# Attention and ELU layers in one kernel: one block transpose for two heads, chunk outputs and small elementwise steps moved to ScalarE

## The chip, the cores and the metric

The kernel runs on one core of a Trainium2 chip. The metric is the device time of one execution in microseconds; the median of three runs is what is compared. The engines are named as in the profile: PE is TensorE, PEld its weight loads, DVE is VectorE, ACT is ScalarE, POOL is GpSimd, SP is SyncE (it only issues DMAs here).

## What is computed

Four batches of eight heads, 768 positions, 64 values a head: attention over a window of 16 positions to either side, joined with 24 block summaries (the maximum of each 32 keys, the mean of each 32 values), then a two-layer network with ELU over all 3072 rows.

```python
k_sum = k.reshape(B, H, nb, 32, D).max(axis=3)
v_sum = v.reshape(B, H, nb, 32, D).mean(axis=3)
scores_l = np.where(abs(i - j) < 16, scale * q @ k.T, -1e9)
scores_s = scale * q @ k_sum.T + log(32)
s = concatenate([scores_l, scores_s], -1)
a = exp(s - s.max(-1)); a = a / (a.sum(-1) + 1e-9)
x = (a @ concatenate([v, v_sum])).reshape(3072, 512)
h = x @ w_in                                   # 512 -> 2048
g = where(h > 0, h, exp(minimum(h, 0)) - 1)
out = g @ w_out                                # 2048 -> 512
```

## The kernel before

The network's matmuls run in a format that keeps fewer bits of a float32, so each operand is split into a high part and the rest, and each product is made of three (high by high, high by rest, rest by high). Rows are worked in six chunks of 512 (`CH`). For each chunk there are sixteen steps `f`, one for each 128 of the 2048 hidden values; step number `n` is `16 * c + f`. A step has these parts:

- `layer1` (L613): 12 matmuls of 512 columns into `h`, from `xh` and `xl`.
- the ELU: `exp_of` (L635) on ScalarE makes `e`; `below` (L640) on VectorE takes min(e, 1) - 1; `above` (L643) on VectorE adds max(h, 0).
- `split_high` (L647) copies `e` to `gh` on ScalarE, `split_rest` (L652) makes `gl` on GpSimd.
- `layer2` (L667): 12 matmuls into the four output banks `o0` to `o3`, from `gh` and `gl`. On TensorE it is issued one step late: the first layer of step n stands ahead of the second layer of step n - 1. At a chunk's last step each bank is finished by itself, copied out and stored (L698 to L700): outputs 0 and 2 by ScalarE, 1 and 3 by VectorE, into borrowed buffers (`cv` twice, `sm`, and the queries' `qbd`).

Attention is worked in groups `g`, twenty of them after those of the start: four steps for a group, which covers two pairs of heads and a third of a batch's rows. At step 2 of four, TensorE makes the values of group g (`group_values`, L570, out of the transposed weights `pt`) and the scores of group g + 1 (`group_scores`, L515). Then the softmax of g + 1 follows for each of its two heads h: `lowest` (L163) on VectorE adds the mask and finds the extreme, `exps` (L173) is four ScalarE passes that also give the sums `z`, `reciprocals` (L181) adds 1e-9 and inverts on VectorE, and `scale_rows` (L185) multiplies on GpSimd. In steps 3, 0 and 1 `group_blocks` (L555) transposes the weights `sm` to `pt` on VectorE, 32 x 32 blocks, 32 instructions a group (11, 11 and 10), issued after the step's `above`. Groups of the first chunk use TensorE for this instead.

Ahead of later batches the block summaries are reduced on VectorE (`summary`, L493) from key and value rows that SyncE loads into two `cv` buffers (`load_summary`, L476); queries and key and value windows of the coming group are loaded by the same queue (`load_group`, L441).

In the first chunk the weights arrive as 64-bit floats and are converted (`Conversion`, L127): a GpSimd pass (`X`), a ScalarE pass (`M`), two VectorE passes (`S`), a ScalarE copy for the high part (`H`, L154) and a GpSimd pass for the rest (`L`, L157). The order of all engines in that chunk is written out by hand in the table `FIRST`, a word for each operation: `E.6` is the exponential of step 6, `ts.6` its `below`, `stt.6` its `above`, `G.6` and `gl.6` its splits, `gz.1.0` the reciprocals of group 1, head 0. After the table, TensorE and SyncE keep the order of the code, and the order on VectorE, ScalarE and GpSimd is made by a scheduler, with `issue_after` as a bound.

Of the kernel before, what the change touches and what calls it, by code (L numbers as in the profile page):

```python
# [26 lines left out]
P = 128  # L27
# [43 lines left out]
    gz.4.0 gz.4.1 gn.4.0 gn.4.1 gb.4.0.8  # L71
# [4 lines left out]
def attn_elu_ffn(ctx: ExitStack, tc: tile.TileContext, qT, kT, vT, v, w_in, w_out, out):  # L76
# [29 lines left out]
    mask = const.tile([P, 3, KC], F32, name="mask")  # L106

# [92 lines left out]
    def new_x(c):  # L200
        xs[c] = (att.tile([P, NP, CH], F32R, tag="xh", name="xh"), att.tile([P, NP, CH], F32R, tag="xl", name="xl"))
# [16 lines left out]
    def first_units():  # L218
# [3 lines left out]
        new_x(0)  # L222
# [18 lines left out]
        v_t = [att.tile([P, UW, row], F32, tag=t, name=f"v{t}") for t in ("xh", "xl")]  # L241
# [295 lines left out]
    def group_low(g, h):  # L537
        th = units[2 * g][0] % NTH
        wide = att.tile([P, UW, P], F32, tag="sm", name="sm")
        sm_of[g, h] = wide[:, :, 0:KC]  # L540
        if g >= NP:
            wide_of[g, h] = wide
            nc.gpsimd.memset(wide[:, :, KC:P], 0.0)
# [8 lines left out]
    def group_transposes(g, h):  # L552
        t_of[g, h] = transposes(sm_of.pop((g, h)), f"a{h}")

    def group_blocks(g, first, end):  # L555

        for i in range(first, end):
            h, (k, q) = i // 16, (x * BLK for x in divmod(i % 16, 4))
            if i % 16 == 0:
                del sm_of[g, h]  # L560
                pt_of[g, h] = att.tile([P, UW, P], F32, tag="pt", name="pt")
            nc.vector.transpose(out=pt_of[g, h][k:k + BLK, :, q:q + BLK], in_=wide_of[g, h][q:q + BLK, :, k:k + BLK])  # L562
            if i % 16 == 15:
                del wide_of[g, h]

    def group_copy(g, h, copy=nc.scalar.copy):
        pt_of[g, h] = att.tile([P, UW, P], F32, tag="pt", name="pt")
        copy(out=pt_of[g, h][0:KC], in_=t_of.pop((g, h))[0:KC])

    def group_values(g):  # L570
# [71 lines left out]

    def above(e, h_ps):  # L643
# [23 lines left out]
    def layer2(c, f):  # L667
# [188 lines left out]
```

## Time and profile before

| | us |
|---|---|
| median of three runs | 620.43 |
| lowest, highest | 617.85, 623.69 |
| the profiled execution | 618.44 |
| its span | 616.7 |
| PE busy | 603.7 |
| DVE busy | 422.4 |
| ACT busy | 256.1 |
| POOL busy | 253.1 |

The profile is of one execution. The span runs from its first to its last instruction; the difference to the execution's own time lies around it. A busy time is the union of an engine's instructions. A timeline row has the start, the length, the engine, the line and the operation, with x and a count where several are joined, and in brackets the idle time before it and what ended that.

### The profile page before, as it was taken

To read this page: it belongs to the slowest core of one execution; us is meant where nothing else is said; L and a number is where in the kernel's file an instruction comes from. 1 tells how busy PE (TensorE), PEld (TensorE's weight loads), DVE (VectorE), ACT (ScalarE), POOL (GpSimd) and SP (SyncE) were. 2 spreads that over 40 slices of the span, in tenths; PEclk is the share of its full clock that TensorE was granted. 3 is DMA by queue.
4 is the path that set the end of the run, shared out by engine and by line. 5 is a ranking of instruction groups with operands and counts; after the bars stand their busy time and mean duration, and the time that the engine had idled before them with its cause. 6 is when DMAs were issued, how large, how long until landed. Compare 5 with 4: busy or idle time off the path is not lost.

```text
span 616.7 us, 11558 instructions
## 1 busy us (share of the span) xinstructions
PE 603.7 (98%) x4123; PEld 490.4 (80%) x4123; DVE 422.4 (68%) x1365; ACT 256.1 (42%) x713; POOL 253.1 (41%) x298
## 2 busy tenths in 40 slices
PE   8999999998999999999999999999999999999997
PEld 6778778886888877888887888888788888888885
DVE  7789987777868878668688697686786774321122
ACT  5858776752332432433424424324243242322222
POOL 4999899842332323323323323233234232122221
PEclk9999999999999999999999999999999999999999
DMA  8998962213105145311053231501311000100001
GB/s 318 332 384 266 306 238 56 59 58 96 48 1 142 53 119 151 97 33 32 2 157 101 74 107 40 143 7 40 111 52 40 2 2 0 69 0 2 1 0 68
DMA packets 63553, 58.65 MB, mean 95 GB/s; under 512 B 22648, under 2 KB 54904, under 8 KB 63496
## 3 DMA queue, kind: packets, MB, share of 16 engines
q1 hardware_dynamic: 60184, 52.02, 27.9%
q10 hardware_dynamic: 3312, 5.90, 2.6%
q8 instruction: 32, 0.52, 0.3%
q14 instruction: 25, 0.20, 0.1%
HBM read 50.82 MB, written 6.29 MB: 93 GB/s over the span
## 4 chain that ended last, share of the span: by engine, by line
PE 67%; DVE 14%; ACT 3%; DMA 2%; issue 2%; SPq 1%; DVEq 0%; ACTq 0%
PE o L674 28%; PE h L621 27%; DVE pt L562 7%; PE h L632 3%; PE o L664 3%; PE o_ps L585 3%; ACT sm L177 2%; PE s L534 2%; DVE e L644 2%; DVE e L641 2%; DMA n<-in_kT_dram 1%; DVE ks L498 1%; DMA vw<-in_v_dram 1%; DVE sh L145 1%; DVE vst L498 1%
## 5 line engine op out<-in xcount | busy, mean ns | idle before, releaser
L654 POOL TENSOR_TENSOR gl<-e,gh 128x512 fp32r<-128x512 f32 x96 | 123.5, 1287 | 239.1 <-issue 133.9
L621 PE MATMUL h<-xh,w 128*128 128x512 f32 x640 | 212.3, 393 | 0.0
L674 PE MATMUL o<-w,gh 128*128 128x512 f32 x648 | 164.5, 390 | 4.0 <-DVE ot L699 2.1
L562 DVE STREAM_TRANSPOSE pt<-sm 32x128 f32<-32x128 f32 x512 | 154.9, 302 | 7.9
L674 PEld LDWEIGHTS o<-w,gh 128*128 128x128 f32 x648 | 121.2, 188 | 31.1 <-DVE ot L699 3.4
L621 PEld LDWEIGHTS h<-xh,w 128*128 128x128 f32 x640 | 120.1, 188 | 27.3 <-issue 2.4
L621 PE MATMUL h<-xl,w 128*128 128x512 f32 x320 | 124.6, 389 | 0.0
L637 ACT ACTIVATE e<-h 128x512 f32<-128x512 f32 x96 | 57.0, 594 | 162.0 <-PE h L621 151.9
L649 ACT CAST gh<-e 128x512 fp32r<-128x512 f32 x96 | 59.6, 621 | 123.4 <-DVE e L644 123.4
L641 DVE TENSOR_SCALAR e<-e 128x512 f32<-128x512 f32 x96 | 46.2, 481 | 92.2 <-ACT e L637 90.5
L674 PE MATMUL o<-w,gl 128*128 128x512 f32 x324 | 89.7, 390 | 0.0
L674 PEld LDWEIGHTS o<-w,gl 128*128 128x128 f32 x324 | 60.8, 188 | 13.0 <-POOL gl L654 0.3
L621 PEld LDWEIGHTS h<-xl,w 128*128 128x128 f32 x320 | 60.1, 188 | 12.0
L177 ACT ACTIVATE sm<-sm,mx 128x120 f32<-128x120 f32 x160 | 61.0, 383 | 19.0 <-DVE mx L169 19.0
L644 DVE SCALAR_TENSOR_TENSOR e<-h,e 128x512 f32<-128x512 f32 x96 | 66.4, 691 | 3.2
L186 POOL TENSOR_TENSOR sm<-sm,z 128x480 f32<-128x480 f32 x40 | 43.2, 1082 | 61.7 <-DVE z L183 53.3
L157 POOL TENSOR_TENSOR w<-cv,w 128x512 fp32r<-128x512 f32 x32 | 41.8, 1320 | 5.3 <-ACT w L154 4.5
L632 PE MATMUL h<-xh,w 128*128 128x512 f32 x120 | 40.5, 399 | 0.0
L599 DVE TENSOR_TENSOR xl<-o_ps,xh 128x256 fp32r<-128x256 f32 x40 | 15.1, 419 | 33.1 <-ACT xh L592 33.1
L169 DVE CUSTOM_DVE_ANT_0 sm<-s,mask 128x120 f32<-128x120 f32 x160 | 34.0, 278 | 1.9 <-PE s L534 1.8
L664 PE MATMUL o<-w,gh 128*128 128x512 f32 x120 | 32.1, 394 | 0.9 <-ACT gh L649 0.9
L177 ACT ACTIVATION_READ_ACCUMULATOR sm<-sm,mx 128x1 f32 x160 | 29.9, 187 | 0.0
(111 smaller groups left out, 529.1 us busy)
## 6 DMA issues: line engine op xcount, KB each, us to landing
raw_w<-in_w_in_dram SPq DMA_DIRECT2D x16, 512.0 KB, 8.1
raw_w<-in_w_out_dram SPq DMA_DIRECT2D x16, 512.0 KB, 9.1
qbd<-in_qT_dram SPq DMA_DIRECT2D x20, 256.0 KB, 2.8
out_dram<-ot ACTq DMA_DIRECT2D x15, 256.0 KB, 2.1
kw<-in_kT_dram SPq DMA_DIRECT2D x24, 144.0 KB, 3.5
vw<-in_v_dram SPq DMA_DIRECT2D x24, 144.0 KB, 3.3
n<-in_kT_dram SPq DMA_DIRECT2D x16, 192.0 KB, 2.4
n<-in_vT_dram SPq DMA_DIRECT2D x16, 192.0 KB, 2.3
```

The costliest lines, as they stand in the source:

```text
L177: nc.scalar.activation(out=sm[:, t, :], in_=sm[:, t, :], func=AF.Exp, bias=mx[:, t, :], scale=-1.0, accum_out=z[:, t, :])
L186: nc.gpsimd.tensor_tensor(out=sm, in0=sm, in1=z.broadcast_to([P, UW, KC]), op=ALU.mult)
L562: nc.vector.transpose(out=pt_of[g, h][k:k + BLK, :, q:q + BLK], in_=wide_of[g, h][q:q + BLK, :, k:k + BLK])
L621: nc.tensor.matmul(h_ps, w[:, a, cols], bb[:, cc, :], start=(k == 0), stop=(k == 3 * NCC - 1))
L632: nc.tensor.matmul(h_ps, w[:, lo, cc * P:(cc + 1) * P], bb[:, cc, :], start=(lo, cc, i) == (0, 0, 0), stop=(lo, cc) == (1, NCC - 1))
L637: nc.scalar.activation(out=e, in_=h_ps, func=AF.Exp)
L641: nc.vector.tensor_scalar(out=e, in0=e, scalar1=1.0, scalar2=-1.0, op0=ALU.min, op1=ALU.add)
L644: top = nc.vector.scalar_tensor_tensor(out=e, in0=h_ps, scalar=0.0, in1=e, op0=ALU.max, op1=ALU.add)
L649: nc.scalar.copy(out=gh, in_=e)
L654: nc.gpsimd.tensor_tensor(out=gl, in0=e, in1=gs[(c, f)][0].bitcast(F32), op=ALU.subtract)
L664: nc.tensor.matmul(o_acc[0][s], gs[(0, f)][a][:, s * P:(s + 1) * P], w[:, bb, :], start=(f, part) == (0, 0), stop=False)
L674: nc.tensor.matmul(o_acc[c][s], a[:, s * P:(s + 1) * P], w[:, bb, :], start=first and f == 0, stop=last and f == NF - 1)
```

## The change

It has five parts. One block transpose covers both heads: `sm` and `pt` become single tiles that hold both heads of a group, a transposition has 256 elements for each partition and there are 16 a group (6, 5 and 5; in a chunk's first step they are issued after the copy of output 1). At chunk ends ScalarE copies outputs 0, 2 and 3, VectorE output 1, all into the `xh` buffer of the finished chunk, and the `x` buffers get a tag for even and for odd chunks. The 1e-9 is added by a ScalarE pass with a bias tile `tiny`. The ELU of steps 6 and 7 is made of a ScalarE pass `gap`, relu(1 - e), and one VectorE pass `larger`, max(-gap, h). `tiny` is first the tile of the activation that warms ScalarE up.

```diff
-    M.15 ge.1.0 S.14 w.21 L2a.5 L2b.5 S.15 E.6 w.22 H.14 L2c.5 X.17 ts.6 H.15 L.14 L1h.7 w.23 M.16 gz.1.0 stt.6
+    M.15 ge.1.0 S.14 w.21 L2a.5 L2b.5 S.15 E.6 gap.6 w.22 H.14 L2c.5 X.17 H.15 L.14 L1h.7 w.23 M.16 gz.1.0 larger.6
...
     def normalize(sm, z):
-        reciprocals(z)
+        nc.vector.reciprocal(out=z, in_=z)
         scale_rows(sm, z)
...
-        xs[c] = (att.tile([P, NP, CH], F32R, tag="xh", name="xh"), att.tile([P, NP, CH], F32R, tag="xl", name="xl"))
+        xs[c] = [att.tile([P, NP, CH], F32R, tag=f"{t}{c % 2}", name=t, bufs=1) for t in ("xh", "xl")]
...
-        warm = const.tile([P, 1], F32, name="warm")
-        nc.vector.memset(warm, 0.0)
-        nc.scalar.activation(out=warm, in_=warm, func=AF.Exp)
+        nc.vector.memset(tiny, 0.0)
+        nc.scalar.activation(out=tiny, in_=tiny, func=AF.Exp)
+        nc.vector.memset(tiny, 1e-9)
...
     def group_exps(g, h):
-        z_of[g, h] = exps(sm_of[g, h], mx_of.pop((g, h)))
+        z_of[g, h] = z = exps(sm_of[g, h], mx_of.pop((g, h)))
+        nc.scalar.activation(out=z, in_=z, func=AF.Identity, bias=tiny)
...
     def group_blocks(g, first, end):
+        if first == 0:
+            for h in range(2):
+                del sm_of[g, h]
+            pt_of[g] = att.tile([P, 2, UW, P], F32, tag="pt", name="pt", bufs=1)
+        src, dst = (a.rearrange("p h t k -> p (h t) k") for a in (wide_of[g], pt_of[g]))
         for i in range(first, end):
-            h, (k, q) = i // 16, (x * BLK for x in divmod(i % 16, 4))
...
-            nc.vector.transpose(out=pt_of[g, h][k:k + BLK, :, q:q + BLK], in_=wide_of[g, h][q:q + BLK, :, k:k + BLK])
+            k, q = (slice(x * BLK, (x + 1) * BLK) for x in divmod(i, P // BLK))
+            nc.vector.transpose(out=dst[k, :, q], in_=src[q, :, k])
...
+    def gap(e):
+        nc.scalar.activation(out=e, in_=e, func=AF.Relu, bias=1.0, scale=-1.0)
+    def larger(e, h_ps):
+        nc.vector.scalar_tensor_tensor(out=e, in0=e, scalar=-1.0, in1=h_ps, op0=ALU.mult, op1=ALU.max)
...
             if not last_chunk:
-                if t < 2:
-                    ot = ffn.tile([P, DO], F32, tag="cv", name="ot", bufs=2)
...
-                (nc.vector.tensor_copy if t % 2 else nc.scalar.copy)(out=ot, in_=o_acc[c][t])
-                nc.scalar.dma_start(out=out[r:r + P, :], in_=ot)
+                if t == 1:
+                    copied = nc.vector.tensor_copy(out=ots[:, t, :], in_=o_acc[c][t]).ins
+                else:
+                    nc.scalar.copy(out=ots[:, t, :], in_=o_acc[c][t])
+                nc.scalar.dma_start(out=out[r:r + P, :], in_=ots[:, t, :])
...
-            if step != 2 and n < 4 * NG - 1:
+            if n % NF and step != 2 and n < 4 * NG - 1:
                 with tc.issue_after(turn):
                     if step == 3:
-                        group_blocks(g + 1, 0, 11)
-                    elif step == 0:
-                        group_blocks(g, 8 if g == NP else 11, 22)
+                        group_blocks(g + 1, 0, 6)
                     else:
-                        group_blocks(g, 22, 32)
+                        group_blocks(g, *(6, 11) if step == 0 else (8 if g == NP else 11, 16))
...
-                layer2(*divmod(n - 1, NF))
+                copied = layer2(*divmod(n - 1, NF))
+            if n % NF == 0 and g < NG:
+                with tc.issue_after(copied):
+                    group_blocks(g, *(0, 8) if g == NP else (6, 11))
```

VectorE at the end of the second chunk, before (L641 and L644 are the ELU's passes, `ot` and `qbd_70` the borrowed output buffers):

```order
L562 STREAM_TRANSPOSE pt<-sm 32x4x32 x11
L641 TENSOR_SCALAR e<-e 128x512
L644 SCALAR_TENSOR_TENSOR e<-h,e 128x512
L562 STREAM_TRANSPOSE pt<-sm 32x4x32 x11
L699 COPY ot<-o_2009 128x512
L699 COPY qbd_70<-o_2011 128x512
L641 TENSOR_SCALAR e<-e 128x512
```

The same place after (L652 and L663 are the ELU's passes, `ots` is the output tile in the `xh` buffer):

```order
L577 STREAM_TRANSPOSE pt<-sm 32x8x32 x6
L652 TENSOR_SCALAR e<-e 128x512
L663 SCALAR_TENSOR_TENSOR e<-h,e 128x512
L712 COPY ots<-o_1980 128x512
L577 STREAM_TRANSPOSE pt<-sm 32x8x32 x5
L652 TENSOR_SCALAR e<-e 128x512
```

The copy of output 1 stands ahead of the transposes, and that of output 3 has left the engine.

ScalarE at the same chunk end, before (L637 is the exponential, L649 the copy to `gh`):

```order
L637 ACTIVATE e<-h 128x512
L699 COPY ot<-o_2008 128x512
L700 DMA out_dram<-ot 128x512
L649 CAST gh<-e 128x512
L699 COPY ot<-o_2010 128x512
L700 DMA out_dram<-ot 128x512 x2
L700 DMA out_dram<-qbd_70 128x512
```

And after (L648 is the exponential, L668 the copy to `gh`):

```order
L648 ACTIVATE e<-h 128x512
L714 COPY ots<-o_1979 128x512
L715 DMA out_dram<-ots 128x512
L668 CAST gh<-e 128x512
L714 COPY ots<-o_1981 128x512
L715 DMA out_dram<-ots 128x512
L714 COPY ots<-o_1982 128x512
L715 DMA out_dram<-ots 128x512 x2
```

Output 3 is copied by ScalarE behind output 2, and the four DMAs are issued by the same queue as before.

VectorE at step 6 of the first chunk, before and after in one piece each (`sh` and `cv` are the weight conversion's joins, `z` the sums of group 1):

```order
L148 SCALAR_TENSOR_TENSOR cv<-raw_w_8_856,sh 128x512
L641 TENSOR_SCALAR e<-e 128x512
L182 TENSOR_SCALAR z<-z 128x4
L183 RECIPROCAL z<-z 128x4
L644 SCALAR_TENSOR_TENSOR e<-h,e 128x512
```

After (L660 is `larger`, L765 the reciprocal):

```order
L149 SCALAR_TENSOR_TENSOR cv<-raw_w_8_856,sh 128x512
L765 RECIPROCAL z<-z 128x4
L660 SCALAR_TENSOR_TENSOR e<-e,h 128x512
```

The two passes with one input have left the engine; their work is done by ScalarE, ahead of its weight copies.

## Rows read from the trace of the kernel before

**Rows 1.** The page: the span, and each engine's busy time and share.

```profile
span 616.7 us, 11558 instructions
...
PE 603.7 (98%) x4123; PEld 490.4 (80%) x4123; DVE 422.4 (68%) x1365; ACT 256.1 (42%) x713; POOL 253.1 (41%) x298
```

**Rows 2.** Waits of TensorE: who waited for whom, total, times, longest, in us.

```profile
PE o L674 <- DVE ot L699: 2.1, 3, 0.9
PE o L674 <- DVE qbd L699: 1.2, 1, 1.2
...
PE s L534 <- DMA kw<-in_kT_dram: 0.9, 1, 0.9
PE o L664 <- ACT gh L649: 0.9, 1, 0.9
PE o L674 <- ACT ot L699: 0.7, 1, 0.7
```

**Rows 3.** Timeline of all engines at the second chunk's end.

```profile
237.18 3.48 DVE L562 STREAM_TRANSPOSE pt<-sm 32x128 f32<-32x128 f32 x11
...
238.87 0.59 ACT L699 COPY ot<-o 128x512 f32<-128x512 f32 x1 [1.07 <-DVE pt L562]
...
239.96 0.61 PE L674 MATMUL o<-w,gh 128*128 128x512 f32 x2
...
240.69 0.69 DVE L699 COPY ot<-o 128x512 f32<-128x512 f32 x1
...
241.44 1.67 PE L674 MATMUL o<-w,gh 128*128 128x512 f32 x6 [0.86 <-DVE ot L699]
```

**Rows 4.** Timeline at step 6 of the first chunk: VectorE, GpSimd, ScalarE, TensorE.

```profile
70.32 1.53 DVE L641 TENSOR_SCALAR e<-e 128x512 f32<-128x512 f32 x1
71.77 1.25 DVE L182 TENSOR_SCALAR z<-z 128x4 f32<-128x4 f32 x1
...
70.27 2.73 POOL L157 TENSOR_TENSOR w<-cv,w 128x512 fp32r<-128x512 f32 x2 [0.75 <-ACT w L154]
...
71.02 1.18 ACT L141 ACTIVATE sh<-raw_w 128x512 f32<-128x512 f32 x2
...
72.58 1.07 PE L632 MATMUL h<-xh,w 128*128 128x512 f32 x4
74.52 1.20 PE L664 MATMUL o<-w,gh 128*128 128x512 f32 x4 [0.86 <-ACT gh L649]
75.89 1.20 PE L664 MATMUL o<-w,gl 128*128 128x512 f32 x4 [0.17 <-POOL gl L654]
```

**Rows 5.** Timeline ahead of the wait for key windows: VectorE, SyncE's queue, TensorE.

```profile
213.51 3.48 DVE L562 STREAM_TRANSPOSE pt<-sm 32x128 f32<-32x128 f32 x11
217.03 1.01 DVE L498 TENSOR_REDUCE vst<-n 128x12 f32<-128x384 f32 x2
...
201.86 16.55 SPq L489 DMA_DIRECT2D n<-in_vT_dram  x6
...
225.51 0.64 PE L534 MATMUL s<-kw,qbd 64*64 64x120 f32 x16 [0.88 <-DMA kw<-in_kT_dram]
```

**Rows 6.** Groups by line: count, busy us, mean ns of one, idle before.

```profile
L562 DVE STREAM_TRANSPOSE pt<-sm 32x128 f32<-32x128 f32 x512 | 154.9, 302 | 7.9
...
L599 DVE TENSOR_TENSOR xl<-o_ps,xh 128x256 fp32r<-128x256 f32 x40 | 15.1, 419 | 33.1 <-ACT xh L592 33.1
```

**Rows 7.** Timeline ahead of the third chunk's end: GpSimd and TensorE.

```profile
331.11 1.29 POOL L654 TENSOR_TENSOR gl<-e,gh 128x512 fp32r<-128x512 f32 x1 [0.68 <-ACT gh L649]
...
332.45 0.50 PE L674 MATMUL o<-w,gl 128*128 128x512 f32 x1
```

**Rows 8.** Timeline of the start: ScalarE's warm-up, VectorE's second key maximum.

```profile
3.03 0.20 ACT L274 ACTIVATE warm<-warm 128x1 f32<-128x1 f32 x1
...
6.43 0.95 DVE L330 TENSOR_REDUCE ks<-kn 128x24 f32<-128x768 f32 x1 [0.94 <-DMA kn<-in_kT_dram]
```

**Rows 9.** Busy time in one group's stretch: length, then PE, PEld, DVE, ACT, POOL.

```profile
349.24:373.29 24.05, 24.05 (x161) 19.77 (x161) 19.89 (x69) 8.55 (x26) 7.81 (x9) 1.00 0.28 76
```

More of the change, by code (lines that the diff above doesn't have):

```diff
@@ L106, in attn_elu_ffn @@
     mask = const.tile([P, 3, KC], F32, name="mask")
+    tiny = const.tile([P, 1], F32, name="tiny")
     raws, weights = {}, {}
@@ L218, in first_units @@
     def first_units():
-        new_x(0)
+        v_t = []
+        xs[0] = []
+        for t in ("xh", "xl"):
+            v_t.append(att.tile([P, UW, row], F32, tag=f"{t}1", name=f"v{t}", bufs=1))
+            xs[0].append(att.tile([P, NP, CH], F32R, tag=f"{t}0", name=t, bufs=1))
         new_summaries(0)
@@ L278, in first_units @@
         nc.vector.memset(v_own[1][QW:KB, 1, :], 0.0)
+        both = att.tile([P, 2, KC], F32, tag="sm", name="m", bufs=1)
         for h in range(2):
-            m = att.tile([P, KC], F32, tag="sm", name="m")
+            m = both[:, h]
             nc.gpsimd.memset(m[:, 0:KB], 0.0)
@@ L538, in group_low @@
         th = units[2 * g][0] % NTH
[L539 to L543, printed above, removed]
+        if g not in wide_of:
+            wide_of[g] = att.tile([P, 2, UW, P], F32, tag="sm", name="sm", bufs=1)
+            if g >= NP:
+                nc.gpsimd.memset(wide_of[g][:, :, :, KC:P], 0.0)
+        sm_of[g, h] = wide_of[g][:, h, :, 0:KC]
         mx_of[g, h] = lowest(({0: 0, 2: 0}, {}, {1: 2, 3: 2})[th], s_of.pop((g, h)), sm_of[g, h])
     def group_exps(g, h):
-        z_of[g, h] = exps(sm_of[g, h], mx_of.pop((g, h)))
+        z_of[g, h] = z = exps(sm_of[g, h], mx_of.pop((g, h)))
+        nc.scalar.activation(out=z, in_=z, func=AF.Identity, bias=tiny)
     def group_norm(g, h):
@@ L553, in group_transposes, with group_copy @@
         t_of[g, h] = transposes(sm_of.pop((g, h)), f"a{h}")
-    def group_blocks(g, first, end):
-        for i in range(first, end):
-            h, (k, q) = i // 16, (x * BLK for x in divmod(i % 16, 4))
-            if i % 16 == 0:
-                del sm_of[g, h]
-                pt_of[g, h] = att.tile([P, UW, P], F32, tag="pt", name="pt")
-            nc.vector.transpose(out=pt_of[g, h][k:k + BLK, :, q:q + BLK], in_=wide_of[g, h][q:q + BLK, :, k:k + BLK])
[L563 to L568, printed above, removed]
+        if (g, 1 - h) not in sm_of:
+            del wide_of[g]
+    def group_copy(g, h, copy=nc.scalar.copy):
+        if g not in pt_of:
+            pt_of[g] = att.tile([P, 2, UW, P], F32, tag="pt", name="pt", bufs=1)
+        copy(out=pt_of[g][0:KC, h], in_=t_of.pop((g, h))[0:KC])
+    def group_blocks(g, first, end):
+        if first == 0:
+            for h in range(2):
+                del sm_of[g, h]
+            pt_of[g] = att.tile([P, 2, UW, P], F32, tag="pt", name="pt", bufs=1)
+        src, dst = (a.rearrange("p h t k -> p (h t) k") for a in (wide_of[g], pt_of[g]))
+        for i in range(first, end):
+            k, q = (slice(x * BLK, (x + 1) * BLK) for x in divmod(i, P // BLK))
+            nc.vector.transpose(out=dst[k, :, q], in_=src[q, :, k])
+        if end == 16:
+            del wide_of[g]
     def group_values(g):
@@ L575, in group_values @@
         o_of[g] = psum.tile([P, 2, UT], F32, tag="h", name="o_ps", bufs=2)
-        pt = [pt_of.pop((g, h)) for h in range(2)]
+        pt = pt_of.pop(g)
         for i in range(2):
@@ L684, in layer2 @@
         last_chunk = c == NCH - 1
-        if last_chunk:
-            ots = att.tile([P, NSUB, DO], F32, tag="xh", name="ots")
+        ots = att.tile([P, NSUB, DO], F32, tag=f"xh{c % 2}", name="ots", bufs=1)
         for t in range(NSUB):
@@ L707, in layer2 @@
                     queue.dma_start(out=out[r:r + P, cols], in_=ots[:, t, cols])
+        if not last_chunk:
+            return copied
     NG = len(units) // 2
@@ L744, in attn_elu_ffn @@
             "E": take_exp, "ts": lambda n: below(es[n]), "stt": lambda n: above(es[n], hs[n]),
+            "gap": lambda n: gap(es[n]), "larger": lambda n: larger(es[n], hs[n]),
             "G": lambda n: split_high(0, n, es[n]), "gl": lambda n: split_rest(0, n, es[n]),
             "gsc": group_scores, "glow": group_low, "ge": group_exps,
[L747 to L748 removed]
+            "gz": lambda g, h: nc.vector.reciprocal(out=z_of[g, h], in_=z_of[g, h]), "gn": lambda g, h: scale_rows(sm_of[g, h], z_of.pop((g, h))),
+            "gtr": group_transposes, "gpc": lambda g, h, i: group_copy(g, h, copies[i]),
             "gval": group_values, "gxh": group_high, "gxl": group_rest,
```

14 lines of the change are left out of this document (4 added, 10 removed).

## The prediction

> **What bounds the kernel now.** I read the page first [rows 1]: TensorE is busy for 603.7 of 616.7 us, so no change on the other engines can give more than the 13.0 us in which it is idle. VectorE at 68% and ScalarE at 42% matter only where TensorE waits for them. So the second view was the list of TensorE's waits [rows 2]. Five of them, 2.1 + 1.2 + 0.7 = 4.0 us, are second-layer products (L674) that wait for an output bank to be copied out at a chunk's end, 0.9 us is a second-layer product of the first chunk (L664) that waits for gh, and 0.9 us is a score product that waits for the DMA of the key windows. The rest of the 13.0 us lies in the start and in the last outputs, which the change leaves as they are. The third view was the timeline at these places.
>
> At the second chunk's end [rows 3] VectorE runs eleven block transposes from 237.18 to 240.66 and only then copies output 1 (240.69) and output 3. ScalarE has long copied output 2 (238.87). TensorE starts the next chunk's products at 239.96; two matmuls take 0.61 where one shows 0.39, so one starts every 0.22 to 0.23, and the third, due at 240.42, comes at 241.44. The wait is marked 0.86 and costs 1.02: each marked wait costs some 0.16 more, because a matmul's end is modelled. The five together then cost 4.0 + 5 x 0.16 = 4.8 us.
>
> In the first chunk [rows 4] the add and minimum of the ELU (L641) takes 1.53 us, over twice the 0.69 of a copy of the same width [rows 3], and the 1e-9 add on only four elements takes 1.25; both lie beside a GpSimd pass over the weights that runs from 70.27 to 73.00. What follows is late: TensorE's four products from 72.58 would be followed at 73.49, and the next come at 74.52 and, for gl, at 75.89 instead of 75.43: 1.03 + 0.46 = 1.5 us.
>
> At 225.51 the score products wait for key windows [rows 5]. SyncE's queue stood still in front of that load: six loads of value rows took it 16.55 us, because each pair needs a buffer that a VectorE reduction frees, and the reduction at 217.03 stands behind eleven transposes.
>
> **The change part by part.**
>
> *Transposes of both heads.* 512 instructions of 0.302 us [rows 6] become 256 of twice the width; the trace shows none of 256 elements. From below: VectorE's ordinary f32 pass over 256 elements takes 0.419. From above: twice 0.302, 0.604. I take 0.45, because a transposition of 128 elements at 0.302 must already hold a fixed part beside its elements, and the row of equal width is the nearest. A group's 16 then take 7.2 us in place of 32 x 0.302 = 9.7. In the 24.05 us of a group [rows 9] TensorE is busy throughout and VectorE for 19.89: the gain of 2.5 us lies beside matmuls and is worth nothing directly. If that cover were gone (VectorE over 24.05 us a group), every further microsecond would count.
>
> *Chunk ends.* In the order, the copy of output 1 now stands ahead of the transposes, and ScalarE has outputs 0, 2 and 3. ScalarE's new copy takes the 0.59 of its old one and stands right behind that of output 2; moved to [rows 3] it would end at 238.87 + 0.59 + 0.59 = 240.05, while output 3 is wanted three pairs of matmuls after 239.96, at 241.3. Cover of over 1 us, so all five waits go: -4.8 us. Bounds: -4.8 and 0 (all copies late again, the second rival).
>
> *1e-9 on ScalarE.* Forty adds leave VectorE; forty small ScalarE passes come, nearest rows 0.20 for one element [rows 8] and 0.59 for 512 [rows 3]; I take 0.25. In the steady stage the first stands ahead of the exponential of the next step and the second behind it, and the reciprocal of the second head now stands between the two VectorE passes of the ELU. So gh and gl of that step come some 0.25 + 0.2 = 0.45 us later. An ordinary step has room for that (two layer passes). Ahead of a chunk end there is none: gl is finished at 331.11 + 1.29 = 332.40 and its product was due at 332.39 [rows 7]. Such a step stands ahead of four chunk ends; I count one as fully hit and one as partly, +0.6 us. Bounds 0 and 4 x (0.59 + 0.2) = +3.2.
>
> A rule of the Trainium skill speaks against this part and the next: ScalarE: Activation LUTs, section Rules for kernel authors, sends relu, min and add to VectorE and not to ScalarE. By it the term of steps 6 and 7 would be 0 instead of -0.8 and the sum 0.8 us worse. The rows disagree at the one place that counts: there VectorE's own pass took 1.53 us.
>
> *ELU of steps 6 and 7.* ScalarE gains a pass of 0.59 and the small add before its two weight copies and two exponent passes, the last of which now end at 71.02 + 1.18 = 72.20 [rows 4]; they move to about 73.0, and gh follows at once, done near 73.6 where it was done near 74.5. On VectorE both slow instructions are gone, so its part is done by about 71.3 (70.32, a reciprocal and one pass of 0.69). But the GpSimd passes over the weights wait for these same copies, move from 73.00 to about 73.8, and gl can be done only at 75.1, 0.7 after its product is due. Of the 1.5 us some 0.8 goes: -0.8. Bounds: -1.5 (GpSimd not held up) and +0.5 (ScalarE, now longer by two passes, is late for weights too).
>
> *Reductions and key windows.* The transposes ahead of the reduction shrink from 3.48 us [rows 5] to 5 x 0.45 = 2.3, and some of those of the step before run behind a reduction. So the buffers come free 1.2 us or more earlier, and SyncE's queue with them. Of 0.9 us I take -0.8; bounds -0.9 and 0.
>
> *Buffers.* One sm and one pt tile of double size replace two of each; the next group's first use comes a step after the last transposition, so no wait is added. The outputs leave cv, sm and qbd for the x tiles of their own chunk, wanted again two steps later. Nothing.
>
> *Start.* A second memset on VectorE waits for ScalarE's first activation, done at 3.03 + 0.20 = 3.23 [rows 8]. Behind it stand the margins, the masks and the key maxima; the second of those waited for a DMA until 6.43 anyway. I take +0.1; bounds 0 and +1.0.
>
> **The sum.** -4.8 + 0.6 - 0.8 - 0.8 + 0.1 = -5.7 us. The profiled execution took 618.44 us (span 616.7 and 1.74 around it), so 612.7. The three timed runs have a median of 620.43, 2.0 higher; the same step from there gives 614.7. I predict the middle, 613.7. All the terms at their best: -4.8 - 1.5 - 0.9 = -7.2.
>
> **The rivals.**
> *All of the small waits go.* If GpSimd isn't held up and gl keeps its time, the gain is near 7.0 us: 611.4 to 613.4. For it: VectorE has less to do everywhere. Against it: GpSimd is behind ScalarE's copies at step 6.
> *The waits pass to ScalarE.* Its second and third copy stand behind gh, gh behind VectorE's ELU, and that now behind transposes which wait for both heads' scaling on GpSimd. If that chain is over 1 us later than in [rows 3], the next chunk's products wait for ScalarE at four ends, some 0.9 each: -5.7 + 3.6 = -2.1, so 616.3 to 618.3. Against it: the cover shown above.
> *VectorE becomes the bound.* Without its transposes a group asks 19.89 - 9.7 = 10.2 us of VectorE [rows 6, 9], which leaves (24.05 - 10.2) / 16 = 0.87 us for one of the new ones. Above that TensorE waits in each of 16 groups: at 1.0 us, 16 x 16 x 0.13 = 33 us slower, less the 5.7: some 646. For it: no such width in the trace. Against it: 0.87 is nearly three times the row for half the width.
>
> **How the numbers follow.** Forecast 0.70, all waits go 0.13, waits pass to ScalarE 0.13, VectorE the bound 0.04. Over 1%, about what a measurement of this kernel can tell from no change, is 6.2 us: the forecast's 5.7, uncertain by about one, passes it 4 times in 10, 0.28 faster and 0.42 within 1%. The first rival adds 0.13 faster, the second 0.13 within, the third 0.04 slower: 0.41, 0.55, 0.04. The range runs from 609.5 (the best sum, a run at the low end of the three) to 618.5 (the second rival from the median).
>
> **What would show it.** Right: no TensorE wait for a copied output in the list, except the last chunk's; the copy of output 1 ahead of the transposes; a transposition of 0.42 to 0.5 us; 1.5 us at step 6 shrunk to about 0.7, now for gl alone; no wait for key windows near 225 us. Wrong: a wait of L674's successor for ScalarE's copies or for gl at every chunk end; TensorE's waits in the middle of groups for pt; a first score product later than before; one table load becoming many.

## The result and the profile after

| | before | changed |
|---|---|---|
| median, first rounds | 620.30 us (617.85 to 623.69, 4 runs) | 611.72 us (610.62 to 611.94, 4 runs) |
| ratio | | 0.9854, 95% interval 0.9806 to 0.9903 |
| median, later rounds (e9) | 619.82 us (617.83 to 620.72, 9 runs) | 611.83 us (611.11 to 613.09, 5 runs) |
| ratio | | 0.9875, 95% interval 0.9857 to 0.9893 |
| profiled execution, span | 618.44, 616.7 us | 611.64, 609.9 us |

By medians the change is faster by 1.2 to 1.5%, and both intervals lie below 1. Trace against trace it is 6.8 us, where the prediction's sum was 5.7. The page of the changed kernel, which answers to [rows 1]:

```profile
span 609.9 us, 11220 instructions
...
PE 601.7 (99%) x4123; PEld 490.4 (80%) x4123; DVE 372.0 (61%) x1063; ACT 267.6 (44%) x760; POOL 247.7 (41%) x282
```

TensorE's idle time fell from 13.0 to 8.2 us and its busy time by another 2.0, so the 13.0 us were not the strict limit that the prediction took them for. VectorE lost 50 us of work. TensorE's waits, in answer to [rows 2]:

```profile
PE o L683 <- POOL gl L673: 0.7, 2, 0.6
PE s L352 <- DMA qn<-in_qT_dram: 0.6, 1, 0.6
PE o L693 <- ACT gh L668: 0.5, 1, 0.5
```

No second-layer product waits for a copied output any more, and no score product for key windows. Behind the start, what is left is gl at step 6, and one new wait for gh. The groups, in answer to [rows 6]:

```profile
L577 DVE STREAM_TRANSPOSE pt<-sm 32x256 f32<-32x256 f32 x256 | 111.6, 436 | 9.2 <-POOL sm L187 5.1
L652 DVE TENSOR_SCALAR e<-e 128x512 f32<-128x512 f32 x94 | 52.5, 559 | 123.1 <-ACT e L648 122.5
...
L553 ACT ACTIVATE z<-z,tiny 128x4 f32<-128x4 f32 x40 | 11.5, 287 | 0.3
```

A wide transposition takes 0.436 us (0.45 was taken). The ELU's first VectorE pass (L652) has become slower, from 0.481 us on average to 0.559; e4 shows why. The second chunk's end, in answer to [rows 3] (VectorE, ScalarE, TensorE):

```profile
232.51 0.68 DVE L712 COPY ots<-o 128x512 f32<-128x512 f32 x1
233.23 2.24 DVE L577 STREAM_TRANSPOSE pt<-sm 32x256 f32<-32x256 f32 x5
...
233.64 0.59 ACT L714 COPY ots<-o 128x512 f32<-128x512 f32 x1
234.12 5.02 ACTq L715 DMA_DIRECT2D out_dram<-ots  x2
239.24 0.60 ACT L648 ACTIVATE e<-h 128x512 f32<-128x512 f32 x1 [5.02 <-DMA kw<-in_kT_dram]
...
235.63 1.98 PE L693 MATMUL o<-w,gh 128*128 128x512 f32 x8
...
241.73 0.97 PE L693 MATMUL o<-w,gh 128*128 128x512 f32 x3 [0.50 <-ACT gh L668]
```

All copies are done by 234.23, over a microsecond before the products at 235.63 want the banks. But the last two output transfers stood 5.02 us in ScalarE's queue, the exponential behind them came at 239.24, and gh a step later was late. Step 6, in answer to [rows 4], and the stretch ahead of the key windows, in answer to [rows 5]:

```profile
70.47 0.17 DVE L765 RECIPROCAL z<-z 128x4 f32<-128x4 f32 x1
70.87 0.69 DVE L660 SCALAR_TENSOR_TENSOR e<-e,h 128x512 f32<-128x512 f32 x1 [0.23 <-ACT e L656]
...
71.43 2.55 POOL L158 TENSOR_TENSOR w<-cv,w 128x512 fp32r<-128x512 f32 x2 [1.96 <-ACT w L155]
73.95 1.28 POOL L673 TENSOR_TENSOR gl<-e,gh 128x512 fp32r<-128x512 f32 x1
...
73.59 1.14 PE L683 MATMUL o<-w,gh 128*128 128x512 f32 x4
75.29 0.97 PE L683 MATMUL o<-w,gl 128*128 128x512 f32 x3 [0.55 <-POOL gl L673]
```

```profile
213.50 2.27 DVE L577 STREAM_TRANSPOSE pt<-sm 32x256 f32<-32x256 f32 x5
215.80 1.01 DVE L503 TENSOR_REDUCE vst<-n 128x12 f32<-128x384 f32 x2
...
220.76 1.05 PE L539 MATMUL s<-kw,qbd 64*64 64x120 f32 x32
```

gh comes in time, gl does not, as forecast. The reduction stands behind five transposes of 2.27 us, not eleven of 3.48, and the 32 score products run without a break.

**Where the time went.** All kernels here run the same 4,123 matmuls in the same order, so a matmul's start (counted from the first matmul) can be set against the start of the same matmul in the kernel before. The difference is its lag. The table gives the lag at landmarks, which are named by their times in the kernel before. Each entry is the change of the lag in that stretch, in us, and negative is gained. "First end" is 104.6 to 146.3, "ends 2 to 4" the second chunk end (to 244) and all that lies past 336.7, "key windows" 223.8 to 225.9, "elsewhere" the rest up to 336.7. The last column sums all but the start.

| kernel | median | to 64.4 | step 6, to 78.1 | to 104.6 | first end | ends 2 to 4 | key windows | elsewhere | past 64 us |
|---|---|---|---|---|---|---|---|---|---|
| changed | 611.72 | +0.15 | -0.75 | -0.09 | -2.53 | -3.07 | -1.11 | +0.60 | -6.95 |
| e9 changed, again | 611.83 | +1.72 | -0.77 | -0.07 | -2.54 | -3.05 | -1.11 | +0.48 | -7.05 |
| e1 ends only | 616.82 | +0.58 | +0.01 | -0.01 | -0.42 | -3.07 | -0.46 | +1.35 | -2.59 |
| e11 ends, own tile | 614.16 | +0.28 | 0.00 | -0.02 | -2.53 | -3.07 | +0.02 | +1.06 | -4.55 |
| e2 ends put back | 611.92 | +0.37 | -0.75 | -0.05 | -2.01 | -3.07 | -1.11 | +0.10 | -6.89 |
| e3 order only | 611.96 | +0.74 | -0.74 | -0.11 | -2.30 | -3.03 | -1.11 | +0.15 | -7.15 |
| e10 wide only | 613.21 | +1.11 | +0.02 | -0.03 | -1.99 | -3.07 | -1.11 | -0.21 | -6.40 |
| e4 narrow | 616.75 | +1.43 | -0.76 | -0.07 | -2.53 | -2.95 | -0.16 | +3.26 | -3.21 |
| e6 narrow, 1e-9 back | 611.79 | -0.03 | -1.09 | -0.60 | -2.53 | -3.07 | -0.17 | +0.65 | -6.81 |
| e7 1e-9 back | 610.81 | +0.06 | -1.06 | -0.23 | -2.53 | -3.07 | -1.11 | -0.21 | -8.21 |
| e8 ELU back | 611.16 | +0.57 | -1.39 | -0.08 | -2.54 | -3.04 | -1.11 | +0.21 | -7.95 |
| e12 mixed | 610.58 | +0.01 | -1.38 | -0.58 | -2.53 | -3.07 | -1.11 | -0.21 | -8.89 |
| e5 doubled | 674.99 | +0.13 | -0.75 | -0.04 | -2.54 | +29.82 | -0.33 | +30.64 | +56.79 |

The two executions of the changed kernel agree to 0.1 us past 64 us, but their starts differ by 1.6. So the last column tells kernels apart better than one time does; the other kernels have one trace each. In the rows but e5's, next to nothing but the third and fourth chunk ends is gained or lost past 336.7 us. e5 is slower throughout: 26.65 of its 29.82 lie past 336.7 us, and its smaller entries depend by some 0.2 on the edges. The medians of before were 619.50, 619.43 and 619.82 in the rounds of e1 to e4, e5 to e8 and e9 to e12.

### The profile page after: what moved, and what is told of

Read it like the earlier page. It is cut to its first block, busy times and chain, and to the rows that moved or that the text cites. A ratio compares the mean times of both kernels' runs of the same rounds, so it can differ in the third digit from the quotient of the medians.

```text
span 609.9 us, 11220 instructions
## 1 busy us (share of the span) xinstructions
PE 601.7 (99%) x4123; PEld 490.4 (80%) x4123; DVE 372.0 (61%) x1063; ACT 267.6 (44%) x760; POOL 247.7 (41%) x282
## 4 chain that ended last, share of the span: by engine, by line
PE 88%; DMA 4%; POOL 3%; DVE 2%; ACT 1%; issue 1%; SPq 0%; ACTq 0%; POOLq 0%; DVEq 0%
PE h L632 35%; PE o L693 35%; PE h L643 5%; PE o L683 5%; PE o_ps L596 3%; PE s L539 3%; DMA qn<-in_qT_dram 1%; DMA kw<-in_kT_dram 1%; POOL w L158 1%; DMA raw_w<-in_w_in_dram 1%; DMA kn<-in_kT_dram 1%; PE t_ps L196 1%; POOL raw_w L137 0%; DVE ks L503 0%; POOL gl L673 0%
## 5 line engine op out<-in xcount | busy, mean ns | idle before, releaser
L652 DVE TENSOR_SCALAR e<-e 128x512 f32<-128x512 f32 x94 | 52.5, 559 | 123.1 <-ACT e L648 122.5
L648 ACT ACTIVATE e<-h 128x512 f32<-128x512 f32 x96 | 56.9, 593 | 158.1 <-PE h L632 129.9
L577 DVE STREAM_TRANSPOSE pt<-sm 32x256 f32<-32x256 f32 x256 | 111.6, 436 | 9.2 <-POOL sm L187 5.1
L668 ACT CAST gh<-e 128x512 fp32r<-128x512 f32 x96 | 59.5, 620 | 112.3 <-DVE e L663 112.0
L187 POOL TENSOR_TENSOR sm<-sm,z 128x480 f32<-128x480 f32 x40 | 39.4, 988 | 80.5 <-DVE z L190 79.9
L663 DVE SCALAR_TENSOR_TENSOR e<-h,e 128x512 f32<-128x512 f32 x94 | 65.0, 692 | 2.7
```

What stands on the lines that cost most here:

```text
L577: nc.vector.transpose(out=dst[k, :, q], in_=src[q, :, k])
L648: nc.scalar.activation(out=e, in_=h_ps, func=AF.Exp)
L652: nc.vector.tensor_scalar(out=e, in0=e, scalar1=1.0, scalar2=-1.0, op0=ALU.min, op1=ALU.add)
L663: top = nc.vector.scalar_tensor_tensor(out=e, in0=h_ps, scalar=0.0, in1=e, op0=ALU.max, op1=ALU.add)
L668: nc.scalar.copy(out=gh, in_=e)
```

## The experiments

**e1, e2, e3: is it the chunk ends?** e1 makes that part alone, in the kernel before:

```diff
-                (nc.vector.tensor_copy if t % 2 else nc.scalar.copy)(out=ot, in_=o_acc[c][t])
+                if t == 1:
+                    copied = nc.vector.tensor_copy(out=ot, in_=o_acc[c][t]).ins
+                else:
+                    nc.scalar.copy(out=ot, in_=o_acc[c][t])
...
+            if n % NF == 0 and g < NG:
+                with tc.issue_after(copied):
+                    group_blocks(g, 0 if g == NP else 11, 22)
```

> The kernel before with the chunk ends alone changed: ScalarE copies outputs 0, 2 and 3, VectorE copies output 1 ahead of its block transposes; transposes (128 elements), ELU and softmax stay as before. Theory (the chunk ends carry most of the gain): the waits of the second-layer products for copied outputs go, 4.8 to 5.6 us, so 4.8 to 5.6 us below the kernel before in the same rounds; the wait at step 6 (1.5 us) and the wait for key windows at 225.5 (0.9 to 1.0 us) stay. Rival (the narrow transposes, now behind the copy, arrive late at the value products, so the wait moves): under 3 us below.

It gave 616.82 us, ratio 0.9957 (0.9944 to 0.9971): 2.7 us, the rival's side. The later ends gave their 3.07 us, the first only 0.42. Its timeline there (VectorE, ScalarE, TensorE):

```profile
137.65 6.94 DVE L562 STREAM_TRANSPOSE pt<-sm 32x128 f32<-32x128 f32 x22
...
142.78 0.58 ACT L702 COPY ot<-o 128x512 f32<-128x512 f32 x1 [1.39 <-DVE pt L562]
...
143.42 1.19 PE L674 MATMUL o<-w,gh 128*128 128x512 f32 x4 [1.82 <-ACT ot L702]
```

The wait has passed to ScalarE's copy of output 2, which writes into an sm tile that the transposes still read. That is the rival's size without its place, since the value products didn't wait. e11 (below) tests it. Of the 1.35 us lost elsewhere, 0.9 lie ahead of the second and third chunk end, where gl is late (waits of 0.29 and 0.20 us), and 0.5 at the score products near 200 us; the ELU's passes there keep their usual 0.43 us, so this is not the slow pass that e4 shows.

e2 leaves the whole change in place but the chunk ends:

```diff
-                if t == 1:
-                    copied = nc.vector.tensor_copy(out=ots[:, t, :], in_=o_acc[c][t]).ins
+                if t % 2:
+                    made = nc.vector.tensor_copy(out=ots[:, t, :], in_=o_acc[c][t]).ins
+                    copied = made if t == 1 else copied
...
-                with tc.issue_after(copied):
+                with tc.issue_after(turn):
```

and issues the transposes ahead of the second layer, as before.

> The changed kernel with its chunk ends put back: VectorE copies outputs 1 and 3 behind its block transposes, ScalarE 0 and 2. Theory 1 (the order at the chunk end alone makes the gain): 5 to 6 us slower than the changed kernel, near 617. Theory 2 (what stands ahead of the copy counts): five transposes of 256 elements are 2.2 us where eleven of 128 were 3.3, so at the second to fourth chunk end the copy of output 1 comes about in time and only the first end, with eight transposes (3.5 us) ahead of the copy, loses: 1 to 2.5 us slower than the changed kernel, 612.7 to 614.2.

It gave 611.92 us (0.9881, 0.9860 to 0.9902), the time of the changed kernel. Theory 1 falls, and the 1 to 2.5 us of theory 2 were too much as well. Its second chunk's end:

```profile
233.59 2.24 DVE L577 STREAM_TRANSPOSE pt<-sm 32x256 f32<-32x256 f32 x5
235.86 1.29 DVE L712 COPY ots<-o 128x512 f32<-128x512 f32 x2
...
236.50 1.98 PE L693 MATMUL o<-w,gh 128*128 128x512 f32 x8
```

Five wide transposes end 1.2 us sooner than eleven narrow ones [rows 3], so even a copy behind them is in time, and the eight products run through. Only the first end loses 0.5 us; that the wait for gh near 245 us (241.73 in the changed kernel's trace) cost 0.17 instead of 0.79 in this execution gives about as much back.

e3 puts output 3 alone back on VectorE, behind the transposes (the first hunk of e2).

> The changed kernel with output 3 copied by VectorE again, behind the transposes; output 1 stays ahead of them. Theory: five transposes (2.2 us) lie between the two copies, so output 3 comes some 0.5 us after its product is due or just in time at the second to fourth end, and up to 1.5 us late at the first, where eight stand between: 0 to 2 us slower than the changed kernel (611.7 to 613.7). Rival (ScalarE's third copy is what delays gh at 241.7, by 0.6 us): 0.5 us faster or more.

611.96 us (0.9879, 0.9858 to 0.9899): no loss that can be measured. By landmarks the first end gives 0.23 less and the wait for gh near 245 us is absent.

**e4, e6, e7: the width, and the 1e-9.** e4 cuts each transposition into its two heads:

```diff
-        for i in range(first, end):
...
-            nc.vector.transpose(out=dst[k, :, q], in_=src[q, :, k])
+        for i in range(2 * first, 2 * end):
...
+            nc.vector.transpose(out=pt_of[g][k, h, :, q], in_=wide_of[g][q, h, :, k])
```

> The changed kernel with each transposition cut into its two heads again: 32 of 128 elements a group, in the same places. VectorE has 2.5 us a group more to do (17.4 to 19.9 of 24.05 us). Theory (VectorE has slack away from the chunk ends, and at these the copy no longer stands behind transposes): within 0.5 us of the changed kernel, but for the wait for key windows at 225.5, which comes back with the eleven transposes ahead of the reduction: 0.5 to 1.2 us slower, 612.2 to 612.9. Rival (the wide transposes are what the gain is made of): over 3 us slower.

616.75 us (0.9956, 0.9940 to 0.9973), the rival's side. The chunk ends stayed cured; what was lost lies in the steps behind a softmax and at the key windows. Ahead of the third chunk's end, in answer to [rows 7] (VectorE, GpSimd, TensorE):

```profile
328.53 1.05 DVE L651 TENSOR_SCALAR e<-e 128x512 f32<-128x512 f32 x1 [0.30 <-ACT e L647]
...
328.31 0.99 POOL L187 TENSOR_TENSOR sm<-sm,z 128x480 f32<-128x480 f32 x1 [4.66 <-DVE z L190]
...
331.10 1.28 POOL L672 TENSOR_TENSOR gl<-e,gh 128x512 fp32r<-128x512 f32 x1 [0.37 <-ACT gh L667]
...
332.43 0.50 PE L692 MATMUL o<-w,gl 128*128 128x512 f32 x1 [0.69 <-POOL gl L672]
```

gl is late and the stretch loses 1.18 us. In the changed kernel the same two stand thus:

```profile
326.11 1.30 POOL L673 TENSOR_TENSOR gl<-e,gh 128x512 fp32r<-128x512 f32 x1 [0.37 <-ACT gh L668]
...
327.65 0.40 PE L693 MATMUL o<-w,gl 128*128 128x512 f32 x1
```

There gl is done 0.24 us early. The VectorE pass of 1.05 us is one of 0.43 that met GpSimd's scaling: it ended 0.28 us after that. A sentence of the Trainium skill bears on this: SBUF — State Buffer, section SBUF: two separate sides, describes a port pair of VectorE and GpSimd that one of them holds for a whole instruction while the other is blocked; the two rows agree in that the pass ended behind GpSimd's, though by less than its own 0.43 us.

The slow passes come with the 1e-9 on ScalarE and not with the width. The ELU's first VectorE pass has a mean of 0.558 to 0.562 us in the changed kernel, e2, e4, e8 and e9, and of 0.461 to 0.482 in before, e6, e7, e10, e11 and e12, where VectorE adds all of the 1e-9 or all but one head's. With wide transposes the pass ahead of the third end takes 1.05 us too, but everything starts early enough for gl.

e6 is e4 with the 1e-9 on VectorE again, e7 the changed kernel with that alone:

```diff
         z_of[g, h] = z = exps(sm_of[g, h], mx_of.pop((g, h)))
-        nc.scalar.activation(out=z, in_=z, func=AF.Identity, bias=tiny)
...
-        nc.vector.reciprocal(out=z, in_=z)
+        reciprocals(z)
```

> The changed kernel with transposes of 128 elements and with the 1e-9 added by VectorE again. Theory (with narrow transposes VectorE reaches a softmax over 2 us later, and ScalarE's add then puts the e of the step behind it beside GpSimd's scaling, 1.05 us in place of 0.43, which made gh and gl late at 208 and 331 us, 0.9 and 1.2 us): these two go, 1.2 to 2.1 us faster than with narrow transposes alone (616.75), 614.6 to 615.6. Rival (the loss with narrow transposes is VectorE's work as such): no change, 616.3 to 617.3.

611.79 us (0.9883, 0.9861 to 0.9905): 5.0 us faster than e4, well past the theory. Past 64 us it is 3.6 of them: 2.6 elsewhere, 0.9 up to 104.6. The other 1.4 lie in the start of the profiled executions, which also differs between two executions of one kernel. But all eight executions of e4 took 616.3 to 617.7 us, so its start may be longer in each of them; that stays open. The rows that answer to e4's:

```profile
323.90 0.43 DVE L650 TENSOR_SCALAR e<-e 128x512 f32<-128x512 f32 x1
...
325.85 1.28 POOL L671 TENSOR_TENSOR gl<-e,gh 128x512 fp32r<-128x512 f32 x1 [0.68 <-ACT gh L666]
...
327.63 0.39 PE L691 MATMUL o<-w,gl 128*128 128x512 f32 x1
```

Here the VectorE pass stands between GpSimd's two scalings, takes 0.43, and gl is 0.50 us early. So narrow transposes cost little by themselves once the order at the chunk ends is new: 1.4 us by landmarks against e7, 0.94 of it at the key windows.

> The changed kernel with the 1e-9 added by VectorE again, wide transposes kept. Theory (the wide transposes bring the softmax forward so that gh and gl have slack whichever engine adds): within 0.5 us of the changed kernel, 611.2 to 612.2. Rival (the add on ScalarE costs the 0.6 us that were predicted for it): 0.6 us or more faster, 611.1 or less.

610.81 us (0.9867, 0.9845 to 0.9888): the rival by its median, but the ratio's interval overlaps that of the changed kernel, so the landmarks must tell. By them the changed kernel is 1.3 us slower: 0.3 at step 6, 0.1 up to 104.6 and 0.8 elsewhere, nearly all of it the wait for gh near 245 us, which stands at 0.59 in e9. That ScalarE's add causes this wait is not shown: e2, e3, e4 and e8 have the add on ScalarE as well, and lose 0 to 0.25 us there. What the add costs lies between 0.4 and 1.3 us.

**e8: the ELU of steps 6 and 7.** Back to VectorE's two instructions (step 6 shown, step 7 alike):

```diff
-    M.15 ge.1.0 S.14 w.21 L2a.5 L2b.5 S.15 E.6 gap.6 w.22 H.14 L2c.5 X.17 H.15 L.14 L1h.7 w.23 M.16 gz.1.0 larger.6
+    M.15 ge.1.0 S.14 w.21 L2a.5 L2b.5 S.15 E.6 w.22 H.14 L2c.5 X.17 ts.6 H.15 L.14 L1h.7 w.23 M.16 gz.1.0 stt.6
```

> The changed kernel with the ELU of steps 6 and 7 in VectorE's two instructions again. Theory: the stall at step 6 (0.7 us between landmarks) comes back, and nothing else: 0.5 to 0.9 us slower, 612.2 to 612.6. Rival: step 7's part counts as well (the value products of the second group came another 0.5 us earlier at 85 us): 1.0 to 1.4 us slower, 612.7 to 613.1.

611.16 us (0.9874, 0.9851 to 0.9898): not slower, so the theory and its rival both fall. Step 6 gains 1.39 us without ScalarE's ELU and 0.75 with it. The stall of before came of two slow VectorE passes beside GpSimd [rows 4], and moving either away clears most of it, since VectorE's SBUF passes are then all but over when GpSimd's pass begins. In e8 (1e-9 moved, ELU not; VectorE, GpSimd, TensorE) the ELU's pass that took 1.53 us takes 0.42, and gl is not waited for:

```profile
70.89 0.42 DVE L652 TENSOR_SCALAR e<-e 128x512 f32<-128x512 f32 x1
...
71.19 2.55 POOL L158 TENSOR_TENSOR w<-cv,w 128x512 fp32r<-128x512 f32 x2 [1.30 <-ACT w L155]
...
75.05 1.19 PE L683 MATMUL o<-w,gl 128*128 128x512 f32 x4
```

In [rows 4] both passes began together, at 70.27 and 70.32 us; here GpSimd's waits for weight copies that ScalarE's added pass has put back, and begins 0.3 us later. In e7 (ELU moved, 1e-9 not) the add that took 1.25 us takes 0.16:

```profile
70.37 0.16 DVE L183 TENSOR_SCALAR z<-z 128x4 f32<-128x4 f32 x1
...
73.53 1.29 POOL L672 TENSOR_TENSOR gl<-e,gh 128x512 fp32r<-128x512 f32 x1
...
74.87 1.21 PE L682 MATMUL o<-w,gl 128*128 128x512 f32 x4 [0.27 <-POOL gl L672]
```

With both moved, ScalarE's two extra passes put back its weight copies, GpSimd waits for these, and gl is late by 0.55.

**e5: how far VectorE is from being the bound.**

```diff
-            nc.vector.transpose(out=dst[k, :, q], in_=src[q, :, k])
+            for _ in range(2):
+                nc.vector.transpose(out=dst[k, :, q], in_=src[q, :, k])
```

> The changed kernel with each block transposition issued twice (32 of 256 elements a group instead of 16; the second writes the same again). 16 x 0.436 = 7.0 us are added to a group, so VectorE has 17.5 + 7.0 = 24.5 us in a group with reductions and 14.5 + 7.0 = 21.5 us in one without, of 24.05. Theory A (only a group's sum counts, the threshold of 0.87 us in the prediction): at most 14 x 0.45 = 6 us slower than the changed kernel, so 612 to 618. Theory B (what stands ahead of the softmax and of each ELU counts, long before VectorE is full): 15 us slower or more, over 627.

674.99 us, ratio 1.0901 (1.0874 to 1.0929): theory B. Waits of TensorE, then its busy time on the page, and one stretch (busy us of PE, PEld, DVE, ACT, POOL, granted clock):

```profile
PE o L694 <- ACT gh L669: 23.9, 18, 3.4
PE o_ps L597 <- DVE pt L578: 15.7, 18, 2.9
```

```profile
PE 624.7 (93%) x4123; PEld 498.0 (74%) x4123; DVE 483.6 (72%) x1319; ACT 265.3 (39%) x760; POOL 247.8 (37%) x282
```

```profile
352.00:378.00 26.00, 23.55 (x118) 18.91 (x114) 21.83 (x61) 9.86 (x31) 7.53 (x8) 0.88 0.25 80
```

VectorE is busy for 72%, below TensorE's 93%, yet 39.6 us are waited for what stands behind its transposes. The same matmuls also take 23 us more, some of it at a lower clock: the granted clock of this stretch is 0.88, between the two levels of 1.2 and 2.4 GHz, so part of it ran at the lower one. It was 1.00 from 360 to 370 us, and 0.74 from 372.5 to 378, behind a wait of 2.45 us that ended at 370.47. At the second and third chunk end the scheduler also set five of the ten transposes, 2.3 us, between the ELU's two passes, so the price is not for the doubled work alone.

**e10, e11, e12: the parts put together.** e10 makes the edits of e2, e7 and e8 at once, so that of the change only the wide transposes and the new tiles are left. e11 is e1 with outputs in a tile of their own:

```diff
...
-                if t < 2:
-                    ot = ffn.tile([P, DO], F32, tag="cv", name="ot", bufs=2)
-                elif t == 2:
-                    ot = att.tile([P, DO], F32, tag="sm", name="ot")
-                else:
-                    ot = qbd[0].rearrange("p t q -> p (t q)")
+                ot = ots[:, t, :]
...
```

> Of the change only the wide transposes and the tiles they need (both heads in one tile, outputs in a tile of their own); chunk ends, ELU of steps 6 and 7 and the 1e-9 as before. Theory (five wide transposes are short enough ahead of VectorE's copies): the chunk ends give 2.0 + 1.2 + 1.27 + 0.6 = 5.1 us, the key windows 1.1, the third chunk's gl 0.2, step 6 nothing: 6.4 us below the kernel before, near 613.0 (612.4 to 613.6). Rival (the order at the chunk ends is needed): under 4 us below, over 615.4.

613.21 us (0.9890, 0.9873 to 0.9907), and 6.40 us by landmarks, as worked out. The tile of their own for the outputs is in these 6.40 as well, and no run has it with narrow transposes and the old order. It can hardly be the cause: four of the five waits of before are for VectorE's copies [rows 2], which stand behind transposes in VectorE's queue, and only one, of 0.7 us, for a copy into the shared sm tile.

> The kernel before with its chunk ends alone changed, and with the outputs copied into a tile of their own instead of into one that the block transposes still read. Theory (ScalarE's copy of output 2 waited 1.4 us for the transposes at the first chunk end, which left 2.1 of its 2.5 us): 1.5 to 2.1 us faster than with the chunk ends alone (616.8), 614.7 to 615.3. Rival (the wait has another cause, such as ScalarE's own queue): no change, 616.3 to 617.3.

614.16 us (0.9905, 0.9889 to 0.9921), 2.7 us faster than e1 by medians, somewhat more than expected, and 2.0 by landmarks. The first end gives its full 2.53, 2.1 more than in e1. The shared tile was the cause.

e12 keeps wide transposes and chunk ends, and has ELU and 1e-9 on VectorE, but for one head:

```diff
-        nc.scalar.activation(out=z, in_=z, func=AF.Identity, bias=tiny)
+        if (g, h) == (1, 0):
+            nc.scalar.activation(out=z, in_=z, func=AF.Identity, bias=tiny)
...
```

> The changed kernel with the ELU of steps 6 and 7 and the 1e-9 on VectorE again, but for the 1e-9 of the second group's first head, which stays on ScalarE. From landmarks: step 6 gives 1.3 us instead of 0.7, the 0.5 us lost at 101 us go, and the wait for gh at 241.7 goes: 0.9 to 1.5 us faster than the changed kernel, 610.2 to 610.9. Rival (ScalarE's share of these edits is worth what it was meant to be): 0.5 us slower or more.

610.58 us (0.9852, 0.9832 to 0.9871), beside 611.83 of the changed kernel in the same rounds; the intervals overlap. By landmarks it is 1.8 to 1.9 us better, the best of all; 0.6 to 0.8 of that is the wait for gh near 245 us, which is absent.

> The changed kernel as it is, in the same rounds as the three others. 611.4 to 612.0 if its first four runs are representative; the wait for gh at 241.7 us (0.6 us), which other runs show at 0 to 0.27, should be absent or smaller in some profiles.

611.83 us (0.9875, 0.9857 to 0.9893), as expected. The wait for gh, 0.59 here, was a little smaller than 0.79 and not gone.

## Why the prediction was right or wrong

The time of 611.72 us lies in the range, 2.0 below the forecast. The range's lower end doesn't follow from its own words, since the lowest run less the best sum, 617.85 - 7.2, is 610.65 and not 609.5. The sum of 5.7 stands against 6.95 to 7.05 by landmarks. It came out near in part by luck: it left out one cure of the chunk-end waits, the wide transposes, but had the other one, the new order, and either is nearly enough.

- **Transposes, the step that failed.** "The gain of 2.5 us lies beside matmuls and is worth nothing directly" is wrong. With their tiles and nothing else they are worth 6.40 us (e10): 5.1 at the chunk ends, where the prediction gave them nothing, and 1.1 at the key windows, where it had seen 0.8. What stands behind the transposes on VectorE starts when they end (in e2 they end at 235.83 us and the copies start at 235.86), so shorter ones bring it forward: the copies at chunk ends and the reduction that frees the key windows' queue. The mean load of a group says nothing of that.
- **Chunk ends.** The mechanism was right and undersized: 2.53 + 3.07 = 5.60, not 4.8. The five marked waits do cost what was worked out, 0.88 + 1.37 + 1.03 + 1.11 + 0.44 = 4.83 by landmarks. Left out was that behind each of them one more matmul is late: it follows the first by 0.34 us instead of 0.23 (in before at 241.44 and 241.78), 0.5 us in all. But the gain is to be had twice. The new order, with the outputs in a tile of their own, gives all of it without wide transposes (e11), and wide transposes give 5.1 of it without the order (e2, e10). On top of them the order is worth 0.5. The "buffers: nothing" was wrong for a kernel with narrow transposes: there the separate output tile is worth 2.1 us (e11 against e1).
- **1e-9 on ScalarE.** The +0.6 was right in sign; 0.4 to 1.3 by landmarks. The place was not: the gl ahead of chunk ends that it was worked out from is late only with narrow transposes (1.18 us in e4, none in e6), and the wide ones take that away. The reason was not either: what the edit does to VectorE is to put the ELU's first pass beside GpSimd's scaling, 0.56 us on average for 0.46 to 0.48. The part of the cost that is shown, 0.4 us, lies at step 6 and up to 104.6; the wait for gh behind the second end, which no row of before shows, may be another cause's.
- **ELU of steps 6 and 7.** Step 6 gave 0.75 of the forecast 0.8, and for the reason given, gl held up behind ScalarE's copies. What was not seen is that either edit alone does better (1.39 with the 1e-9 edit in e8, 1.06 with the ELU edit in e7), so that the ELU edit costs 0.64 on top of the other. By the rule of the Trainium skill that the prediction set aside (ScalarE: Activation LUTs, section Rules for kernel authors) this pass belongs on VectorE; beside the other edit the runs agree with it.
- **Key windows.** -0.8 forecast, -1.11 measured, by the mechanism named; with narrow transposes only 0.16 of it is had (e4).
- **Start.** +0.1 forecast. +0.15 and +1.72 in two executions of the same kernel, so one execution can't tell.
- **The rivals.** The size is that of the first rival (near 7.0), without its reason: GpSimd was held up. ScalarE's copies are waited for nowhere in the changed kernel, against the second rival. The third rival's price was wrong: at twice 0.436, just past the 0.87 us from which TensorE was to wait, the cost is 63 us (39.6 of it in two kinds of wait, 23 in longer matmuls), since the wait depends on what stands behind the transposes, long before VectorE is full.
- **The base.** Between medians the gain is 8.0 to 8.6 us, 1.0 to 1.6 more than by landmarks. The granted clock of each execution goes with that. Of the 35 executions of before in the rounds of e1 to e12, the 17 at 0.999 or 1.000 have a median of 618.69 us and the 18 below that 620.3. Of the changed kernel's nine, the seven at 1.000 have a median of 611.64, and the two at 0.997 took 612.75 and 613.09. At like clocks the gain is 7.05 us, or 1.1%, which is that of the landmarks. In e9, one of the two at 0.997, the difference lies in the first 64 us. Why before has the lower clock more often stays open, since it has one trace, at 1.000.

## What to carry to other kernels

An instruction on an engine that is "hidden" by its mean load still sets when everything behind it in that engine's queue starts: cost an edit at nothing only after looking at what stands next in the queue and who waits for it. Where several edits cure one stall, try each alone and each left out, since the second cure is worth nothing or costs. Compare traces at the same matmuls, so that a start that varies doesn't hide a gain of a few tenths of a per cent.

## What the runs showed of the hardware

- The start varies with nothing changed. Here are the first 64 us of the changed kernel, first the execution of e9, then the first one (columns as in e5):

```profile
0.00:64.00 64.00, 59.30 (x643) 46.89 (x644) 51.02 (x165) 44.95 (x133) 51.17 (x87) 0.97 0.97 324
```

```profile
0.00:64.00 64.00, 60.78 (x676) 46.90 (x676) 51.90 (x167) 45.64 (x134) 52.30 (x91) 1.00 0.98 329
```

  In e9 the granted clock of the stretch was 0.97 instead of 1.00 (0.83 from 14 to 20 us), and 33 fewer matmuls were done. TensorE waited 1.3 us for the first queries instead of 0.6, and besides 0.7 us for a key maximum and 1.1 us for converted weights, of which the first execution shows neither.
- Two output transfers held ScalarE's queue for 5.02 us (4.94 in e9, 4.54 in e8, 2.48 in e12, 2.05 in e7, 2.00 in e4), and its compute instructions behind them waited. In the first trace the profile names a load of key windows, issued from SyncE, as what the exponential behind them waited for, in e9 a matmul; what held the queue is not shown. Issuing the outputs from another queue was not tried.
- A block transposition of 256 elements takes 0.436 us where 128 take 0.302: 0.134 us for 128 more elements. On a straight line through these two points, which is an estimate, some 0.17 us are paid by every one.
